# A decay-attention and mixture-of-experts kernel: the state sum as a product with the identity, the router's constants and choices at another place, another first load, and the last group in two pieces

## Chip, cores and metric

The kernel runs on one core of one Trainium2 chip. The metric is the device time of one execution in microseconds (us), as the median of several executions.

## The reference

Two parts follow one another. The first is a linear attention with a complex decay (4 batches, 8 heads, 768 tokens, 48 features a head). The second is a mixture of 8 experts in which each of the 3072 tokens goes to one expert, in the order of the logits, and each expert takes at most 384 tokens.

```python
mag = np.sqrt(a_re * a_re + a_im * a_im)
scale = np.minimum(mag, 0.999) / (mag + 1e-06)
a_re_n, a_im_n = (a_re * scale, a_im * scale)
for t in range(S):
    new_re = ar * S_re - ai * S_im
    new_im = ar * S_im + ai * S_re
    S_re, S_im = (new_re + kv, new_im)
    y[:, :, t] = np.einsum('bhd,bhde->bhe', q[:, :, t], S_re)
...
logits = x @ w_gate
order = np.argsort(-logits.flatten())
for idx in order:
    tok, e = (int(idx) // E, int(idx) % E)
    if assigned[tok] >= 0 or counts[e] >= cap:
        continue
    assigned[tok] = e
    counts[e] += 1
for e in range(E):
    h = np.maximum(x[assigned == e] @ w1[e], 0.0)
    out[assigned == e] = h @ w2[e]
```

## The kernel before

**Attention in chunks.** The tokens of a batch are cut into six chunks of 128. A *unit* is one chunk with all 8 heads, so there are 24 units, 0 to 23; batch 3 is units 18 to 23. In the code `i` is the unit and `cc` its place in the batch (0 to 5). Three units are a *group* (8 groups, 0 to 7; groups 6 and 7 are batch 3). For a whole group `elementwise` works the decays out: squares, logarithms, exponentials and sines on ScalarE (ACT), products, prefix sums (the scans `zi` and `neg`) on VectorE (DVE), with tiles `ar`, `ai`, `s`, `p`, `neg`, `zi`, `CS`, `kq`. `CUTS` lets a group be done in pieces; before, group 0 alone is (one chunk, then two). `PLAN` says, for each piece, in which of the alternating loads of ACT's function tables its four stages lie.

**Rotation and restacking.** `turns` multiplies keys and then queries of a unit by cosine and sine: two DVE instructions `f<-kq,CS` of 768 elements, the second of which makes the unit ready. `stack` then issues eight transfers `KQ<-f` on the queue of SyncE (SP), which take the parts of `f` to the layout that TensorE (PE) needs.

**A unit on PE.** `unit` makes the scores `sc`, which DVE masks (`am`, two instructions a unit); for `cc` below 5 it transposes the keys (`kp`, copied by ACT to `kt`) and multiplies them with the values into `U`, the chunk's own contribution to the state. Before, each head's product is 96 columns wide, of which 48 are its own. For `cc` of 1 to 4, DVE adds the state of the chunks ahead (`tmp<-U,W`) and multiplies the sum with the chunk's decay (`W<-tmp,KQ`); for `cc` of 0 one instruction `W<-U,KQ` does it. Two tiles `W` take turns. `mix` makes `y` from `am` and the values and from the queries and the state; ACT copies it to `xT`, PE turns it and multiplies it with the gate's weights in the same step (`xp<-pick,xT`), ACT copies `x` out to memory `xd`, and DVE reduces the logits (`lg<-xp`).

**Router.** After a batch, `best` chooses the best expert for the batch's six tiles of tokens (five DVE instructions over 48 elements, the first `top<-lg`, the last `oh<-q,qm`). The last batch's lot is done in `Router.scale`, behind attention. `Router.constants` is a list of small pieces (`masks`, `levels`, and five `level`s of four tiny DVE instructions on two partitions, `sa`, `sb`, `sb`, `steps`), handed to `attention` as `later`. With the last logits the search for each expert's threshold starts (`find`, tiles `ind`, `cnt`, `thr`), and then the experts' products (`acc`).

**What sets the order.** In attention every piece of work is an `Op` with an engine, a cost and a priority: `at` (the unit's number, or near it) plus an offset for its kind from the table `OFF`. `in_order` plays these Ops through a list scheduler, which on each engine takes the ready Op of the lowest priority, and emits them in that order; an idle engine takes whatever is ready. All engines then work strictly in this order, the SP queue too. The functions `dve`, `dve2`, `sca` and the numbers in `op(...)` are the costs by which it plans. The experts' part has a planner of its own, which the change doesn't touch. The instructions carry line 131, that of a helper, so they are told apart by their tiles.

Of the kernel before, what the change touches and what calls it, by code (L numbers as in the profile page):

```python
# [24 lines left out]
GC = 3  # L25
# [24 lines left out]
def constants(nc, con, z, w_gate):  # L50
    v, g = nc.vector, nc.gpsimd

    def t(n, shape, dt=F32):
        x = con.tile(shape, dt, name=n)
        setattr(z, n, x)
        return x

    jp = t("jp", [128, 128], I32)
    g.iota(jp, pattern=[[1, 128]], base=0, channel_multiplier=-1)
    v.tensor_scalar(t("ident", [128, 128]), jp, 0.0, None, op0=OP.is_equal)  # L60
    v.tensor_scalar(t("mask", [128, 128]), jp, 0.0, None, op0=OP.is_ge)
# [12 lines left out]
    t("cidx", [128, NT])  # L74
    t("pid", [128, 1])
    pick = t("pick", [128, 4, 104])
    v.memset(pick, 0.0)
    for s in range(2):
        r = slice(64 * s, 64 * s + 48)
        v.tensor_copy(pick[r, :, 48 * s:48 * s + 48], z.ident[r, None, r].to_broadcast([48, 4, 48]))  # L80
        nc.sync.dma_start(pick[r, :, 96:104], w_gate[:, s].rearrange("p d e -> d p e"))
    t("lg", [128, NT, E])
    t("top", [128, NT])
    t("qm", [128, NT])
    t("oh", [128, NT, E], BF)
    t("ext", [128, 2, B])
# [149 lines left out]
def attention(nc, real, tc, z, q, k, a_re, a_im, v_tok, xd, later):  # L236
# [35 lines left out]
        return o  # L272

    def dve(n):
        return n / 960 + 0.069

    def scan_(n):
        return n * 2.15 / 960 + 0.06

    def dve2(n):  # L280
        return n / 1920 + 0.069

    def sca(n, bias=False):
        return n / 1200 + (0.187 if bias else 0.093)

    def pool(n):
        return n / 460 + 0.08
# [53 lines left out]
    def elementwise(gi, j, at):  # L341
# [114 lines left out]
    def unit(i):  # L456
# [11 lines left out]
        for hh in range(2):  # L468
            def scores(hh=hh):
                sc = ps.tile([128, 4, 128], F32, name="sc", bufs=2)  # L470
                mine["sc", hh] = sc
                for h in range(4):
                    nc.tensor.matmul(sc[:, h], KQ()[:, hh * 4 + h, :128], KQ()[:, hh * 4 + h, 128:256], start=True, stop=True)

            def mask(hh=hh):
                a = wk.tile([128, 4, 128], F32, name="am", bufs=4)
                v.tensor_tensor(a, mine["sc", hh], z.mask[:, None].to_broadcast([128, 4, 128]), op=OP.mult)
                mine["am", hh] = a
            op(("SC", i, hh), "pe", 0.875, at - 0.5, scores, KD + [("MK", i - 1, hh)])
            op(("MK", i, hh), "dve", 0.602, at, mask, [("SC", i, hh), ("MX", i - 2)])  # L480
        if cc < 5:
            for hh in range(2):
                def flip(hh=hh):
                    kp = ps.tile([128, 4, 96], F32, name="kp", bufs=2)
                    mine["kp", hh] = kp
                    for h in range(4):
                        nc.tensor.transpose(kp[:, h], KQ()[:, hh * 4 + h, :128], z.ident[:96, :96])

                def copy(hh=hh):
                    if "kt" not in mine:  # L490
                        mine["kt"] = wk.tile([128, 8, 96], F32, name="kt")
                    nc.scalar.activation(mine["kt"][:, hh * 4:hh * 4 + 4], mine["kp", hh], AF.Copy)
                op(("FL", i, hh), "pe", 0.36, at - 0.45, flip, KD + [("KC", i - 1, hh), ("KC", i - 2, hh)])
                op(("KC", i, hh), "act", 0.38, at, copy, [("FL", i, hh), ("ST", i - 2), ("ST", i - 3)])
# [12 lines left out]

            def nxt():
                return W[(cc + 1) % 2][:, :384].rearrange("p (a b) -> p a b", a=8)
            if cc:  # L510
                def add_():
                    tmp = wk.tile([96, 8, 48], F32, name="tmp", bufs=1)
                    mine["tmp"] = tmp
                    v.tensor_tensor(tmp.rearrange("p a b -> p (a b)"), mine["U"][:, :384], W[cc % 2][:, :384], op=OP.add)
                op(("UA", i), "dve", 0.469, at - 0.1, add_, [("ST", i), ("WM", i - 1), ("WM", i - 2)])
                op(("WM", i), "dve", 0.47, at, lambda: v.tensor_tensor(nxt(), mine["tmp"], gate(), op=OP.mult),
                   [("UA", i), ("MX", i - 1)])
            else:
                op(("UA", i), "dve", 0.469, at - 0.1,
                   lambda: v.tensor_tensor(nxt(), mine["U"][:, :384].rearrange("p (a b) -> p a b", a=8), gate(), op=OP.mult),  # L520
                   [("ST", i), ("MX", i - 1), ("WM", i - 2), ("UA", i - 2), ("MX", i - 2)])
                made["WM", i] = made["UA", i]

        def mix():
            Wc = W[cc % 2]
# [40 lines left out]
        op(("MX", i), "pe", 2.2 if cc else 1.18, at, mix,  # L566
           [("MK", i, 0), ("MK", i, 1), ("lv", gi), ("XC", i - 1)] + ([("WM", i - 1)] if cc else []))
        op(("XC", i), "act", 0.478, at - 0.1, evac, [("MX", i), ("FN", i - 2)])
        op(("FN", i), "pe", 0.70, at + 0.6, turn, [("XC", i), ("XE", i - 2), ("LR", i - 2)])
        op(("XE", i), "act", 0.41, at, out, [("FN", i), ("XS", i - 2)])  # L570
        op(("XS", i), "dma", 0.546, at, store, [("XE", i)])
        op(("LR", i), "dve", 0.13 if i % 6 < 5 else 0.98, at, logits, [("FN", i)])

    def load(key, cost, at, fn, deps=()):
        op(key, "dma", cost, at, fn, deps)
# [803 lines left out]
```

## Time and profile before

Three executions took 545.6, 545.8 and 547.11 us, median 545.8. The profile is of a further execution.

| | us |
|---|---|
| the profiled execution's own time | 550.18 |
| its span, first to last instruction | 548.4 |
| busy PE / DVE / ACT / GpSimd (POOL) | 445.6 / 437.1 / 276.5 / 72.9 |
| mean granted TensorE clock | 0.923 |

The page's rows of tenths cut the span into 40 slices of 13.7 us. Row "PE" is the share in which a product was under way, "PEclk" the TensorE clock granted (9 and above is full, 5 is half). A timeline row is: start, duration, engine, line, instruction, tiles written and read, shape, count, and in brackets the idle time ahead of it with what ended it. A windows row is: the stretch, its length, and for each engine its busy time and its instructions, then the granted clock, the share of the DMA engines and the GB/s. A row of the groups ends in the busy time of all and the mean ns of one. SPq and ACTq rows are the issue of transfers. On PE most single-precision products stand as two records, so x16 are eight products.

### The profile page before, as it was taken

The numbers are of one execution on the slowest core, as the hardware profiler recorded it, in microseconds if no ns is written. First come the engines' busy times: TensorE is split into PE (matmuls) and PEld (weight loads), VectorE is DVE, ScalarE is ACT, GpSimd is POOL, SyncE is SP. The second block draws the span as 40 slices with busy tenths as digits, with TensorE's granted clock in tenths as the row PEclk, the third lists the DMA queues.
The fourth block names the chain that finished last, engine by engine and source line by source line (L and its number), as shares of the span: only waits on it lengthen the run. The fifth ranks groups of instructions, "written<-read, shape, count | busy, mean of one in ns | idle before, by whom it ended". The sixth has DMA issues, their size and how long they took to land. (4 is left out here: it accounts for less than half of the span.)

```text
span 548.4 us, 9215 instructions
## 1 busy us (share of the span) xinstructions
PE 445.6 (81%) x3383; PEld 392.6 (72%) x3383; DVE 437.1 (80%) x1267; ACT 276.5 (50%) x422; POOL 72.9 (13%) x87
## 2 busy tenths in 40 slices
PE   0005997699679967995489899999999999999994
PEld 0005996599678856994375458887889888999993
DVE  7999999979899989944667768889899898965240
ACT  5997579828887688322012513244172432834231
POOL 1000000000000000000121311332132223460102
PEclk9999999579859995998569999999999999999999
DMA  8625867578756885541071513245062431950001
GB/s 240 234 76 140 240 200 240 140 193 215 247 155 178 242 276 154 136 120 45 0 274 48 208 47 131 78 177 221 30 244 73 159 130 39 393 189 16 30 14 43
DMA packets 47596, 82.47 MB, mean 150 GB/s; under 512 B 5568, under 2 KB 43200, under 8 KB 45504
## 3 DMA queue, kind: packets, MB, share of 16 engines
q1 hardware_dynamic: 38720, 42.57, 27.2%
q0 software_dynamic: 5376, 34.61, 16.9%
q10 hardware_dynamic: 3456, 4.72, 2.5%
q8 instruction: 26, 0.43, 0.3%
q14 instruction: 18, 0.15, 0.1%
HBM read 53.49 MB, written 9.44 MB: 115 GB/s over the span
## 5 line engine op out<-in xcount | busy, mean ns | idle before, releaser
L131 PE MATMUL sc<-KQ 96*128 96x128 f32 x384 | 60.3, 317 | 41.6 <-DMA KQ<-f 40.7
L131 PEld LDWEIGHTS sc<-KQ 96*128 96x128 f32 x384 | 55.2, 226 | 44.0 <-DMA KQ<-f 41.6
L131 ACT ACTIVATE hh<-acc 128x384 fp32r<-128x384 f32 (+1 forms) x64 | 30.6, 490 | 75.2 <-PE acc L131 75.0
L131 PE MATMUL acc<-w2h,hl 128*128 128x384 f32 x168 | 55.1, 346 | 0.0
L131 PE MATMUL acc<-w2l,hh 128*128 128x384 f32 x168 | 54.9, 345 | 0.0
L131 PE MATMUL acc<-w2h,hh 128*128 128x384 f32 x168 | 54.4, 343 | 0.0
L131 PE MATMUL acc<-xh,w1h 128*128 128x384 f32 x168 | 53.6, 347 | 0.3 <-DVE idx L131 0.2
L131 PE MATMUL acc<-xl,w1h 128*128 128x384 f32 x168 | 53.1, 345 | 0.0
L131 PE MATMUL acc<-xh,w1l 128*128 128x384 f32 x168 | 52.6, 343 | 0.0
L131 POOL DMA_INDIRECT w1t<-in_w,eidx x8 | 8.8, 1099 | 312.4 <-DVE of L131 269.3
L131 ACT ACTIVATE ot<-acc 128x384 f32<-128x384 f32 x24 | 11.8, 492 | 70.7 <-PE acc L131 55.8
L131 DVE TENSOR_TENSOR f<-kq,CS 128x768 f32<-128x768 f32 x48 | 43.7, 949 | 0.9 <-ACT CS L131 0.9
L131 DVE SCALAR_TENSOR_TENSOR hl<-acc,hh 128x384 fp32r<-128x384 f32 x56 | 30.4, 551 | 15.9 <-ACT hh L131 15.3
L131 PE MATMUL y<-am,V 128*64 128x128 f32 x384 | 38.0, 288 | 3.0 <-DVE am L131 2.0
L131 DVE TENSOR_TENSOR ind<-m,thr 128x768 bf16<-128x768 f32 (+1 forms) x40 | 33.7, 849 | 6.9 <-PE thr L131 6.6
L131 PE MATMUL kp<-ident,KQ 96*128 96x96 f32 x160 | 25.0, 301 | 15.7 <-DMA KQ<-f 9.5
L131 POOL DMA_INDIRECT out<-ot,idx x24 | 25.3, 1053 | 93.2 <-ACT ot L131 82.9
L131 DVE TENSOR_TENSOR am<-sc,mask 128x512 f32<-128x512 f32 x48 | 31.5, 680 | 6.2 <-PE sc L131 6.1
L131 PE MATMUL U<-V,kt 128*96 128x96 f32 x320 | 35.2, 270 | 0.9 <-DVE tmp L131 0.9
L131 POOL DMA_INDIRECT xg<-xd,idx x24 | 28.1, 1172 | 57.1 <-DVE idx L131 29.4
L131 PEld LDWEIGHTS U<-V,kt 128*96 128x96 f32 x320 | 33.1, 184 | 2.7 <-issue 1.2
L131 PE MATMUL xp<-pick,xT 112*128 112x104 f32 x192 | 25.9, 285 | 10.7 <-ACT xT L131 8.5
(195 smaller groups left out, 1082.7 us busy)
## 6 DMA issues: line engine op xcount, KB each, us to landing
KQ<-f SPq DMA_DIRECT2D x192, 96.4 KB, 2.2
V<-in_v SPq DMA_DIRECT2D x8, 576.0 KB, 4.8
kq<-in_k SPq DMA_DIRECT2D x8, 576.0 KB, 6.6
kq<-in_q SPq DMA_DIRECT2D x8, 576.0 KB, 7.8
xd<-x ACTq DMA_DIRECT2D x24, 192.0 KB, 3.0
ai<-in_a_im SPq DMA_DIRECT2D x7, 576.0 KB, 4.4
ar<-in_a_re SPq DMA_DIRECT2D x7, 576.0 KB, 5.1
ai<-in_a_im SPq DMA_DIRECT2D x1, 384.0 KB, 3.6
```

Of the source, the lines that this page charges most:

```text
L131: r = f(*a, **k)
```

## The change

Five things in the code, and the table of offsets.

- **State sum on PE.** `state` multiplies each head with its own 48 columns, into a `U` of 384 columns, and leaves the sum open; for `cc` of 1 to 4 a new Op `CA` multiplies the old state `W` (96 x 384) with the identity into the same `U`. DVE's `tmp<-U,W` is gone, and `W<-U,KQ` reads `U` for every unit. `U` is then free only when `W<-U,KQ` is done.
- **Router.** The priority of `later` goes from 3.0 to 23.0, and `best` for the first three batches becomes one Op over 18 tiles (144 elements), `BE`, with priority 25.
- **Loads.** A group's `ar` no longer waits for its `ai` in the plan, and the two small transfers of `w_gate` go from SP's queue to GpSimd's.
- **Last group.** `CUTS` cuts group 7 into its first two chunks and its last one, and `PLAN` has ten entries with 20 table loads instead of nine with 22.
- **Planning costs** are somewhat higher for DVE and ACT, and every offset in `OFF` has another value.

```diff
-        nc.sync.dma_start(pick[r, :, 96:104], w_gate[:, s].rearrange("p d e -> d p e"))
+        g.dma_start(pick[r, :, 96:104], w_gate[:, s].rearrange("p d e -> d p e"))
...
-CUTS = {0: [(0, 1), (1, GC)]}
+CUTS = {0: [(0, 1), (1, GC)], 7: [(0, 2), (2, GC)]}
...
     def dve(n):
-        return n / 960 + 0.069
+        return n / 960 + 0.1
...
-        add("la", "dma", dma(128 * N3 * 4), load_a(gi, j, "ar", a_re), free("ar", ["F1", "F3", "F4"], gi) + k_("li"))
+        add("la", "dma", dma(128 * N3 * 4), load_a(gi, j, "ar", a_re), free("ar", ["F1", "F3", "F4"], gi))
...
             def state():
-                Wc = W[cc % 2]
-                U = ps.tile([96, 432], F32, name="U")
+                U = ps.tile([96, 384], F32, name="U")
                 mine["U"] = U
                 for h in range(8):
-                    nc.tensor.matmul(U[:, h * 48:h * 48 + 96], mine["kt"][:, h], v_[:, c, h * 48:h * 48 + 96],
-                                     start=True, stop=True)
-            op(("ST", i), "pe", 1.33, at - 0.2, state, [("KC", i, 0), ("KC", i, 1), ("lv", gi), ("UA", i - 1), ("UA", i - 2)])
+                    nc.tensor.matmul(U[:, h * 48:h * 48 + 48], mine["kt"][:, h], v_[:, c, h * 48:h * 48 + 48],
+                                     start=(h == 0), stop=(h == 7 and not cc), skip_group_check=True)
+
+            def carry():
+                nc.tensor.matmul(mine["U"], z.ident[:96, :96], W[cc % 2][:, :384], start=False, stop=True,
+                                 skip_group_check=True)
+            op(("ST", i), "pe", 1.33, at - 0.2, state, [("KC", i, 0), ("KC", i, 1), ("lv", gi), ("WM", i - 1), ("WM", i - 2)])
+            if cc:
+                op(("CA", i), "pe", 0.65, at - 0.1, carry, [("ST", i), ("WM", i - 1), ("WM", i - 2)])
+            else:
+                made["CA", i] = made["ST", i]
...
-            if cc:
-                def add_():
-                    tmp = wk.tile([96, 8, 48], F32, name="tmp", bufs=1)
-                    mine["tmp"] = tmp
-                    v.tensor_tensor(tmp.rearrange("p a b -> p (a b)"), mine["U"][:, :384], W[cc % 2][:, :384], op=OP.add)
-                op(("UA", i), "dve", 0.469, at - 0.1, add_, [("ST", i), ("WM", i - 1), ("WM", i - 2)])
-                op(("WM", i), "dve", 0.47, at, lambda: v.tensor_tensor(nxt(), mine["tmp"], gate(), op=OP.mult),
-                   [("UA", i), ("MX", i - 1)])
...
+            op(("WM", i), "dve", 0.52, at,
+               lambda: v.tensor_tensor(nxt(), mine["U"].rearrange("p (a b) -> p a b", a=8), gate(), op=OP.mult),
+               [("CA", i), ("MX", i - 1), ("CA", i - 1)])
...
-                if i + 1 < NT:
-                    best(nc, z, wk, z.lg[:, r], z.top[:, r], z.qm[:, r], z.oh[:, r])
...
-        op(("later", n), "dve", 0.6, 3.0, lambda fn=fn: fn(nc), [("later", n - 1)])
-    made["LR", 5].deps.append(made["later", len(later) - 1])
+        op(("later", n), "dve", 1.0, NT - 1.0, lambda fn=fn: fn(nc), [("later", n - 1)])
+
+    def choices():
+        r = slice(0, NT - 6)
+        best(nc, z, wk, z.lg[:, r], z.top[:, r], z.qm[:, r], z.oh[:, r])
+    op(("BE", 0), "dve", 1.5, NT + 1.0, choices, [("LR", i) for i in range(NT - 6)] + [("later", len(later) - 1)])
...
-PLAN = [(0, 0, 1, 3), (0, 2, 1, 3), (2, 4, 3, 5), (4, 6, 5, 7), (6, 8, 7, 9), (8, 10, 9, 11), (10, 12, 11, 13), (14, 16, 15, 17), (18, 20, 19, 21)]
+PLAN = [(0, 0, 1, 3), (0, 2, 1, 3), (2, 4, 3, 5), (4, 6, 5, 7), (6, 8, 7, 9), (8, 10, 9, 11), (10, 12, 11, 13), (12, 14, 13, 15), (14, 16, 15, 17), (16, 18, 17, 19)]
```

Where rows stand now is shown at three places. In these rows a shape like 128x3x128 is partitions by elements, and x2 is a run of two alike.

The start of SP's queue (`V` are the values, `kq` keys and queries), before:

```order
L131 DMA ai<-in_a_im 128x3x128
L131 DMA ai<-in_a_im 128x3x256
L81 DMA pick<-in_w_gate 48x4x8 x2
L131 DMA V_114<-in_v 128x3x384
L131 DMA ar<-in_a_re 128x3x128
L131 DMA ar<-in_a_re 128x3x256
```

and in the changed kernel:

```order
L131 DMA ar<-in_a_re 128x3x128
L131 DMA ar<-in_a_re 128x3x256
L131 DMA ai<-in_a_im 128x3x128
L131 DMA ai<-in_a_im 128x3x256
L131 DMA V_114<-in_v 128x3x384
```

`ar` now goes first, and the gate's weights have left the queue.

The start of DVE's real work in the changed kernel. Before, all five `level`s stand ahead of the first row that needs a load, `p<-ar,ai`:

```order
L131 TENSOR_SCALAR start<-jf 1x32
L131 TENSOR_SCALAR pidm<-pid 32x1
L131 TENSOR_SCALAR neg<-ar 128x3x128
L131 TENSOR_SCALAR sa<-jf 2x32
L131 TENSOR_SCALAR sb<-jf 2x32
L131 TENSOR_TENSOR sb<-sb,sa 2x32
L131 SCALAR_TENSOR_TENSOR steps<-sb,row,sa 2x32
L131 TENSOR_SCALAR neg<-ar 128x3x256
```

The `level`s now stand singly among the first groups' work, all of them within the first two groups, though their priority says the end of attention.

DVE around the rotations of units 18 to 20, before (the first row of three holds both of unit 18 and one of unit 19; `zi`, `p`, `neg` and the second `kq` are group 7's):

```order
L131 TENSOR_TENSOR f<-kq,CS 128x6x128 x3
L131 TENSOR_SCALAR zi<-s_1755 128x1152
L131 TENSOR_TENSOR f<-kq,CS 128x6x128
L131 TENSOR_TENSOR p<-p,s_1806 128x1152
L131 SCALAR_TENSOR_TENSOR zi<-zi,s_1755 128x128 x9
L131 SCALAR_TENSOR_TENSOR neg<-p,tl,neg 128x384 x3
L131 TENSOR_TENSOR f<-kq,CS 128x6x128
L131 TENSOR_TENSOR kq<-kq,zi 128x1152
L131 TENSOR_SCALAR neg<-neg 128x1152
L131 TENSOR_TENSOR f<-kq,CS 128x6x128
```

and in the changed kernel (the rows of `p` are group 7's first piece; `W` and `am` belong to units 16 and 17):

```order
L131 TENSOR_TENSOR f<-kq,CS 128x6x128 x3
L131 TENSOR_TENSOR W_112<-U,KQ 96x384
L131 TENSOR_TENSOR am<-sc,mask 128x512 x2
L131 TENSOR_TENSOR f<-kq,CS 128x6x128
L131 TENSOR_TENSOR p<-p,s_1666 128x3x256
L131 TENSOR_TENSOR f<-kq,CS 128x6x128 x2
```

The prefix sums and most of group 7's other work now stand behind unit 20's second rotation.

DVE ahead of the last two rotations (unit 23's) in the changed kernel; the `W` is unit 20's:

```order
L131 TENSOR_SCALAR neg<-neg 128x3x128
L131 TENSOR_TENSOR W_112<-U,KQ 96x384
L131 TENSOR_TENSOR kq<-kq,s_1706 128x3x128
L131 TENSOR_REDUCE top<-lg 128x18
L131 TENSOR_TENSOR q_2204<-lg,top 128x144
L131 TENSOR_TENSOR q_2204<-q_2204,wd 128x144
L131 TENSOR_REDUCE qm<-q_2204 128x18
L131 TENSOR_TENSOR oh<-q_2204,qm 128x144
L131 TENSOR_TENSOR f<-kq,CS 128x6x128 x2
```

Unit 23's rotations now wait, in DVE's order, for a `W` that waits for PE, and for the choices of the first 18 tiles.

More of the change, by code (lines that the diff above doesn't have):

```diff
@@ L280, in dve2 @@
     def dve2(n):
-        return n / 1920 + 0.069
+        return n / 1920 + 0.11
     def sca(n, bias=False):
-        return n / 1200 + (0.187 if bias else 0.093)
+        return n / 1200 + (0.23 if bias else 0.14)
     def pool(n):
@@ L478, in mask @@
                 mine["am", hh] = a
-            op(("SC", i, hh), "pe", 0.875, at - 0.5, scores, KD + [("MK", i - 1, hh)])
-            op(("MK", i, hh), "dve", 0.602, at, mask, [("SC", i, hh), ("MX", i - 2)])
+            op(("SC", i, hh), "pe", 0.9, at - 0.5, scores, KD + [("MK", i - 1, hh)])
+            op(("MK", i, hh), "dve", 0.64, at, mask, [("SC", i, hh), ("MX", i - 2)])
         if cc < 5:
@@ L492, in copy @@
                     nc.scalar.activation(mine["kt"][:, hh * 4:hh * 4 + 4], mine["kp", hh], AF.Copy)
-                op(("FL", i, hh), "pe", 0.36, at - 0.45, flip, KD + [("KC", i - 1, hh), ("KC", i - 2, hh)])
-                op(("KC", i, hh), "act", 0.38, at, copy, [("FL", i, hh), ("ST", i - 2), ("ST", i - 3)])
+                op(("FL", i, hh), "pe", 0.34, at - 0.45, flip, KD + [("KC", i - 1, hh), ("KC", i - 2, hh)])
+                op(("KC", i, hh), "act", 0.44, at, copy, [("FL", i, hh), ("ST", i - 2), ("ST", i - 3)])
             def state():
-                Wc = W[cc % 2]
-                U = ps.tile([96, 432], F32, name="U")
+                U = ps.tile([96, 384], F32, name="U")
                 mine["U"] = U
                 for h in range(8):
-                    nc.tensor.matmul(U[:, h * 48:h * 48 + 96], mine["kt"][:, h], v_[:, c, h * 48:h * 48 + 96],
-                                     start=True, stop=True)
-            op(("ST", i), "pe", 1.33, at - 0.2, state, [("KC", i, 0), ("KC", i, 1), ("lv", gi), ("UA", i - 1), ("UA", i - 2)])
+                    nc.tensor.matmul(U[:, h * 48:h * 48 + 48], mine["kt"][:, h], v_[:, c, h * 48:h * 48 + 48],
[8 more added lines that the diff above has]
+                made["CA", i] = made["ST", i]
             def gate():
@@ L509, in nxt @@
                 return W[(cc + 1) % 2][:, :384].rearrange("p (a b) -> p a b", a=8)
-            if cc:
-                def add_():
-                    tmp = wk.tile([96, 8, 48], F32, name="tmp", bufs=1)
-                    mine["tmp"] = tmp
-                    v.tensor_tensor(tmp.rearrange("p a b -> p (a b)"), mine["U"][:, :384], W[cc % 2][:, :384], op=OP.add)
-                op(("UA", i), "dve", 0.469, at - 0.1, add_, [("ST", i), ("WM", i - 1), ("WM", i - 2)])
-                op(("WM", i), "dve", 0.47, at, lambda: v.tensor_tensor(nxt(), mine["tmp"], gate(), op=OP.mult),
-                   [("UA", i), ("MX", i - 1)])
[L518 to L522, printed above, removed]
+            op(("WM", i), "dve", 0.52, at,
+               lambda: v.tensor_tensor(nxt(), mine["U"].rearrange("p (a b) -> p a b", a=8), gate(), op=OP.mult),
+               [("CA", i), ("MX", i - 1), ("CA", i - 1)])
         def mix():
@@ L563, in logits @@
                 v.tensor_reduce(z.ext[:, 1, b:b + 1], lg, op=OP.min, axis=AX.X)
-                if i + 1 < NT:
-                    best(nc, z, wk, z.lg[:, r], z.top[:, r], z.qm[:, r], z.oh[:, r])
-        op(("MX", i), "pe", 2.2 if cc else 1.18, at, mix,
+        op(("MX", i), "pe", 1.9 if cc else 1.0, at, mix,
            [("MK", i, 0), ("MK", i, 1), ("lv", gi), ("XC", i - 1)] + ([("WM", i - 1)] if cc else []))
-        op(("XC", i), "act", 0.478, at - 0.1, evac, [("MX", i), ("FN", i - 2)])
-        op(("FN", i), "pe", 0.70, at + 0.6, turn, [("XC", i), ("XE", i - 2), ("LR", i - 2)])
-        op(("XE", i), "act", 0.41, at, out, [("FN", i), ("XS", i - 2)])
+        op(("XC", i), "act", 0.54, at - 0.1, evac, [("MX", i), ("FN", i - 2)])
+        op(("FN", i), "pe", 0.9, at + 0.6, turn, [("XC", i), ("XE", i - 2), ("LR", i - 2)])
+        op(("XE", i), "act", 0.46, at, out, [("FN", i), ("XS", i - 2)])
         op(("XS", i), "dma", 0.546, at, store, [("XE", i)])
-        op(("LR", i), "dve", 0.13 if i % 6 < 5 else 0.98, at, logits, [("FN", i)])
+        op(("LR", i), "dve", 0.15 if i % 6 < 5 else 0.45, at, logits, [("FN", i)])
     def load(key, cost, at, fn, deps=()):
@@ L626 @@
 START = dict(pe=0.0, act=0.6, dve=1.5, pool=3.4, dma=0.0)
-OFF = {"A1": 5.6974, "F1": -7.9403, "F10": -7.0891, "F11": -2.5142, "F2": 4.603, "F3": 2.2139, "F4": 2.5395, "F5": -0.7373, "F6": -7.499, "F7": -8.0, "F8": 8.0, "F9": -4.5957, "FL": -8.0, "FL<": -0.67, "FN": 7.9979, "G1": -0.9278, "G2": -0.7621, "G3": 0.005, "G4": 2.5464, "G5": -8.0, "K": 0.9248, "KC": 8.0, "LR": 8.0, "MK": 3.115, "MX": 3.0055, "N0": -8.0, "N1": -6.1077, "N2": -1.1451, "P0": -1.533, "R0": -1.808, "R1": -6.8663, "R2": -0.3699, "R3": 5.5431, "R4": -2.409, "R5": -7.3329, "S": -8.0, "SC": -7.6492, "SC<": -8.0, "ST": 4.3481, "ST<": -5.7794, "T1": 1.9301, "T2": -8.0, "T3": 2.462, "TL": 3.4506, "UA": -5.175, "UA<": -8.0, "WM": 8.0, "XC": -2.3796, "XC<": 3.7972, "XE": -0.9541, "XS": 8.0, "la": -5.2264, "later": -1.1817, "li": -4.9185, "lk": 6.1616, "lv": 4.0153, "RK": -0.8502, "RQ": -0.8125, "table": -3.9707}
+OFF = {"A1": 6.5218, "F1": -3.963, "F10": -8.0, "F11": -3.7643, "F2": 8.0, "F3": 3.4146, "F4": 6.2286, "F5": -2.6336, "F6": -7.5201, "F7": 2.1619, "F8": -1.0245, "F9": -8.0, "FL": -8.0, "FL<": -7.3946, "FN": 8.0, "G1": 8.0, "G2": -1.285, "G3": 6.3021, "G4": -5.8232, "G5": -3.7953, "K": 0.0172, "KC": -8.0, "LR": 4.482, "MK": -0.7872, "MX": 7.0247, "N0": 0.2966, "N1": -8.0, "N2": -0.2657, "P0": -5.8009, "R0": 6.9605, "R1": 1.4172, "R2": -2.4071, "R3": -0.3573, "R4": 4.9463, "R5": -1.815, "S": -8.0, "SC": 1.5433, "SC<": 3.9494, "ST": -0.4983, "ST<": 8.0, "T1": 0.0502, "T2": -6.6124, "T3": -0.6944, "TL": -2.0259, "UA": -4.4369, "UA<": 5.2541, "WM": -6.1886, "XC": -0.2695, "XC<": 5.8251, "XE": 1.7266, "XS": 4.1758, "la": -8.0, "later": 0.9443, "li": -6.5411, "lk": 8.0, "lv": 7.3515, "RK": -2.6027, "RQ": -2.5432, "table": 7.641, "CA": -5.0223, "BE": 6.7757}
 CHAIN = ("scalar", "vector", "tensor", "gpsimd", "sync")
```

## The prediction

> **What bounds the kernel now.** I read the rows of tenths on the page first, to cut the span into stages.
>
> ```profile
> span 548.4 us, 9215 instructions
> PE   0005997699679967995489899999999999999994
> DVE  7999999979899989944667768889899898965240
> PEclk9999999579859995998569999999999999999999
> ```
>
> DVE is full up to slice 16 (219 us), PE only afterwards. The windows of attention show the change of hands.
>
> ```profile
> 172.00:201.40 29.40, 26.19 (x312) 24.22 (x312) 27.33 (x51) 21.85 (x27) 0.00 (x0) 1.00 0.75 234
> 201.40:227.00 25.60, 19.58 (x149) 17.57 (x150) 24.72 (x42) 18.82 (x23) 0.00 (x0) 0.73 0.61 167
> 227.00:253.40 26.40, 25.48 (x312) 24.11 (x308) 11.57 (x30) 6.96 (x14) 0.00 (x0) 1.00 0.38 102
> ```
>
> Behind the length stand the busy times of PE, its weight loads, DVE, ACT and GpSimd. Up to 227 DVE has work nearly all the time; then PE has 26 us left to do, alone. So attention is a DVE stage with a PE tail, and the tail is as long as batch 3 comes late to PE. The third view is the timeline there.
>
> ```profile
> 200.49 2.69 DVE L131 TENSOR_TENSOR f<-kq,CS 128x768 f32<-128x768 f32 x3
> 215.25 0.95 DVE L131 TENSOR_TENSOR f<-kq,CS 128x768 f32<-128x768 f32 x1
> 220.69 3.55 DVE L131 TENSOR_TENSOR f<-kq,CS 128x768 f32<-128x768 f32 x4
> 253.18 0.19 DVE L131 TENSOR_REDUCE lg<-xp 128x8 f32<-128x32 f32 x1 [0.85 <-ACT x L131]
> 36.96 16.58 SPq L131 DMA_DIRECT2D KQ<-f  x24
> 202.34 36.26 SPq L131 DMA_DIRECT2D KQ<-f  x48
> KQ<-f SPq DMA_DIRECT2D x192, 96.4 KB, 2.2
> ```
>
> Unit 18's second rotation ends at 202.3 (200.49 and two of the three in 2.69), unit 20's at 216.2, unit 21's at 222.4. SP issues the transfers of the six units in one run, from 202.34 to 238.6. One unit's eight take 5.5 us in an earlier run (16.58/3) and land 2.2 later. Attention ends with the last logits at 253.4. The 295.0 us of router and experts behind that are the same rows in the same order in both programs and read nothing that the change makes later, so I leave them as they are.
>
> **The change, term by term**, against the profiled execution.
>
> *The start.* DVE's first row that needs a load waits for `ar`.
>
> ```profile
> 0.75 0.97 SPq L131 DMA_DIRECT2D ai<-in_a_im  x2
> 3.27 1.02 SPq L131 DMA_DIRECT2D ar<-in_a_re  x2
> 3.43 0.52 ACT L131 ACTIVATE s<-ai 128x384 f32<-128x384 f32 x1 [1.40 <-DMA ai<-in_a_im]
> 8.66 0.56 DVE L131 SCALAR_TENSOR_TENSOR p<-ar,ai 128x384 f32<-128x384 f32 x1 [1.48 <-DMA ar<-in_a_re]
> 2.10 0.60 DVE L80 COPY pick<-ident 48x192 f32<-48x192 f32 x2
> 1.03 0.79 POOL L131 MEMSET W<- 96x400 f32 x2
> 2.78 0.23 POOL L131 IOTA jf<- 2x32 f32 x1
> L131 POOL DMA_INDIRECT xg<-xd,idx x24 | 28.1, 1172 | 57.1 <-DVE idx L131 29.4
> ```
>
> What is issued first is there at 3.43, so DVE could begin at 3.4 instead of 8.66. But GpSimd now issues the two transfers of `w_gate`, which wait for `pick`, ahead of its constants, and DVE's `start<-jf` stands ahead of its first `neg<-ar`. This trace has no such issue on GpSimd. The nearest row is the indirect transfer, 1.17 us. Two of them behind `pick` at 2.7 end at 5.0, and the 2.0 us of constants (1.03 to 3.01) bring DVE to 7.0; with nothing for them it is 3.4. I take 6.0, near the row: **-2.7** (-5.3 to -1.7).
>
> *DVE's work ahead of unit 18.*
>
> ```profile
> 189.02 0.55 DVE L131 TENSOR_TENSOR tmp<-U,W 96x384 f32<-96x384 f32 x1
> 189.49 0.75 DVE L131 TENSOR_SCALAR neg<-neg 128x1152 int32<-128x1152 int32 x1
> 228.59 0.19 DVE L131 TENSOR_REDUCE top<-lg 128x6 f32<-128x48 f32 x1
> 229.54 0.21 DVE L131 TENSOR_TENSOR oh<-q,qm 128x48 bf16<-128x48 f32 x1
> 3.26 0.16 DVE L131 TENSOR_SCALAR sa<-jf 2x32 f32<-2x32 f32 x1
> 6.94 0.24 DVE L131 SCALAR_TENSOR_TENSOR steps<-sb,row,sa 2x32 bf16<-2x32 f32 x1
> ```
>
> A sum `tmp` holds DVE for 0.47 us (to the next start); batches 0 to 2 have 12: **-5.6**. A lot of choices takes 1.15 (228.59 to 229.75), and two lots stood ahead: **-2.3**. The five levels took 3.9 us (3.26 to 7.18) in the wait for the first load; in the new order they stand behind it: **+3.9**. Adding start-to-start times row by row through both orders leaves +0.5 for other pieces of group 7 now ahead. Together -6.2: unit 18's second rotation ends near **196.1**.
>
> ACT has two table loads fewer; it was not the last to be waited for at these rows, and I count nothing for them.
>
> *Units 18 to 20.* From there to unit 20's second rotation the new order has four rotations (0.87 each), one `W` (0.47), two masks (0.60 each) and a `p` (0.87): 6.0 us, so **202.1** instead of 216.2. The three sets of transfers go out in one run: unit 18 lands at 203.8 (5.5 and 2.2), unit 20 at 214.3 instead of 223.8.
>
> *Unit 21 on.* Splitting group 7 adds instructions, and the 18 tiles' choices move ahead of unit 23's rotations; unit 21's second rotation has 1.3 us less of work ahead than before, so with the start 218.4 instead of 222.4. SP then issues 24 transfers in 16.6 us, to 235.0, landed at 237.2.
>
> *PE's tail.*
>
> ```profile
> sum 43.50, PE 41.89 PEld 39.56 DVE 29.38 ACT 18.55 POOL 0.00; mean PE 6.98 PEld 6.59 DVE 4.90 ACT 3.09 POOL 0.00
> 209.00:216.00 7.00, 5.63 (x28) 5.26 (x29) 7.00 (x10) 6.11 (x7) 0.00 (x0) 0.50 0.62 173
> 221.80 1.60 PE L131 MATMUL U<-V,kt 128*96 128x96 f32 x16
> 223.23 1.06 PE L131 MATMUL xp<-pick,xT 112*128 112x104 f32 x8
> 224.13 0.82 PE L131 MATMUL kp<-ident,KQ 96*128 96x96 f32 x8
> 224.79 1.98 PE L131 MATMUL sc<-KQ 96*128 96x128 f32 x16
> 248.54 0.44 PE L131 MATMUL y<-am,V 128*64 128x128 f32 x4
> 287.99 1.46 PE L131 MATMUL acc<-xh,w1t 128*128 128x384 f32 x4
> 250.45 2.03 PE L131 MATMUL xp<-pick,xT 112*128 112x104 f32 x16
> 356.91 0.25 PE cnt L131 x6
> ```
>
> From 209 to 252.5, six units took 41.9 us of PE, the first at half clock. `U` takes 1.43 (221.80 to 223.23, where the next product starts). With 48 columns the trace has none: half is 0.72, nothing saved is 1.43. Six `cnt` products of 32 columns, each with its own 128 weights, take 0.25, or 0.04 a load; with two loads a product that gives 0.67. I take 0.75, so -0.7 in five units. The identity product is four times `U`'s width; the same width in single precision takes 0.73 (four records, 1.46), in four units +2.9. Net -0.6 (-0.8 to +2.9). PE can begin at 203.2, as unit 18's first heads land, and is done 41.3 later: **244.5**. By SP's run it is 237.2 and the last unit's mask, `y`, copy, turn and logits: 1.2 and the 4.8 from 248.54 to 253.37, **243.2**. The later of the two, about 244.4, sets the end: **-9.0**. In batches 0 to 2 PE's net change (12 x 0.73 more, 15 x 0.7 less) lies beside DVE's work. `U` has one buffer, now free only after `W`; between one unit's sum and the next unit's `U` stand a `y` (1.9, 248.54 to 250.45) and mostly `sc` on PE, which cover the 0.5 us of `W`; without that cover PE would lose these 0.5 us in each of four units.
>
> The Trainium skill, page "TensorE: Matmul & The Clock Gate", section "LDWEIGHTS (loading the stationary operand)", has a load last its columns divided by 1.2, in ns. For 96 columns, loaded twice, that is an estimated 1.28 us for eight products, so `U` would save only 0.15 and the tail would end 2.7 later, -6.3 in all. The trace speaks against it: the four `kp` products load 128 columns twice each and take 0.66 (224.13 to 224.79), where the rule gives 0.85.
>
> *Sum.* 550.18 - 9.0 = 541.2 for a profiled execution. It stood 4.4 above the median of 545.8, so the median becomes **536.8**.
>
> **Rivals.**
>
> *The `W` rows wait for PE in the tail.* Unit 20's `W` stands ahead of unit 23's rotations. After unit 20 lands at 214.3, PE owes `sc`, `y`, `U`, a turn and the sum, 6.5 us at full clock, so 220.8, and DVE comes there at 221.5. At half clock it is 227.3, and the last rotations come 5.8 later: 232 instead of 226, landed at 240, end 246. With 1 us in each earlier batch the end is near 249, the time **541.5**. For it: the clock of 0.73 from 201 to 227. Against it: PE has two units waiting by then, and from 227 the clock is 1.00.
>
> *GpSimd holds up the start.* If each transfer takes twice the 1.17, `start<-jf` comes at 9.4, 0.7 after today's start instead of 2.7 ahead: **540.2**. The trace shows no such issue beside DVE's copies. The Trainium skill, page "SBUF — State Buffer", section "SBUF: two separate sides", warns of just this: transfers issued from GpSimd starve while DVE copies single-precision tiles, 3.1 us instead of 0.62; by an estimate of 5 us more than nothing for the two it would give about the same time, and no run here shows it so far.
>
> *Slower: every `W` waits for the product, from batch 0.* The state's sum leaves DVE but DVE must now wait, in its order, until PE has done `U` and the sum.
>
> ```profile
> DVE W L131 <- PE U L131: 4.0, 2, 3.1
> sum 165.40, PE 135.65; mean PE 33.91
> ```
>
> Before 227, the `W` that read `U` directly, one a batch, waited 4.0 us in all, 3.1 the longest; averaged over four, 1.0 each. If the 12 new ones wait 1.3 each (4.0 over the three of batches 0 to 2), DVE loses 15.6 us and the time is 536.8 + 15.6 = **552.4**. It is slower than before from 0.75 us each on (9.0/12). For it: at half clock `U` and the sum take 3 us. Against it: in the new order 5 to 9 us of other DVE rows lie between one `W` and the next, and from 36 to 201.4 PE has 29.8 us free.
>
> *It doesn't do what it says.* SP's queue has loads of `V` and `kq` ahead of unit 18's transfers; if one waits for unit 14, those go out no earlier, and the time is **545.8**.
>
> **How the numbers follow.** Forecast 0.50 (its own terms span 532 to 540), tail wait 0.20, GpSimd 0.12, slower 0.13, nothing 0.05. The range takes in the first three, from 531 to 543.5. Faster by over 0.3% (about what a measurement here can tell from no change) are the first three, less a little for their near ends: 0.81; same 0.06; slower 0.13.
>
> **What would show it.** Right: DVE's first row with a load at about 6; unit 18's second rotation near 196 and unit 20's near 202; SP's last run ended by 235; `U` near 0.75 us for eight at full clock; PE without long waits from 204; last logits near 244; router and experts 295 us. Wrong: DVE rows `W` with idle from PE above 0.75 us on average; a wait for `w_gate`; `U` still at 1.4; or PE at half clock beyond 212.

## The result: 1% slower, and where the time went

The changed kernel takes **552.74 us** (552.49 to 554.86, four runs), the kernel before 546.45 on the same chip (545.6 to 548.11): a ratio of **1.0102**, 95% interval 1.0076 to 1.0129. 536.8 was forecast, with a range up to 543.5. The profiled execution took 552.71 and is thus a typical one.

The rows of tenths on the page of the changed kernel come first.

```profile
span 550.9 us, 9282 instructions
PE   0019995899879899998369999999999999999994
DVE  8998889968997967964576888889899898965240
PEclk9999997559956958999559999999999999999998
```

PE mostly has 8s and 9s from the fourth slice on, while DVE, which was full up to the sixteenth, has gaps. In slices 8, 9 and 15 PE has 8 or 9 and its clock row has 5: PE is busy because it is slow. Two windows give the size, one from the middle of attention and one that the prediction used; the columns are as there, and the last three are the granted clock, the DMA share and GB/s.

```profile
100.00:200.00 100.00, 92.06 (x738) 84.49 (x738) 87.33 (x153) 72.62 (x89) 0.00 (x0) 0.74 0.69 192
201.40:227.00 25.60, 25.36 (x232) 22.79 (x232) 19.31 (x40) 12.63 (x22) 0.00 (x0) 0.83 0.60 168
```

The same first window in the kernel before:

```profile
100.00:200.00 100.00, 87.01 (x854) 81.19 (x856) 91.52 (x172) 71.92 (x87) 0.00 (x0) 0.84 0.73 209
```

In these 100 us PE is busy for 5 us more and shows 116 product records fewer, and DVE's busy time falls from 91.5 to 87.3. From 201 to 227 PE is busy nearly throughout (25.36 of 25.60; before 19.58) and DVE for 19.3 us (before 24.7). What DVE waits for stands in the waits of the changed kernel from 3 to 227 us (who waited for whom; us in all, times, longest).

```profile
DVE am L131 <- PE sc L131: 13.5, 9, 4.0
DVE W L131 <- PE U L131: 5.1, 4, 3.6
DVE W L131 <- PE y L131: 2.0, 1, 2.0
```

That is 20.6 us. Before, it was the 4.0 us of `W` and 0.9 us of `tmp`. (The waits of the logits' rows, 1.7 us here and 1.3 before, are left out.) Most of it isn't the wait for the state (`W`) but for the scores (`sc`), ahead of a mask `am` that stands in DVE's row. The timeline shows such places, at 56.81, 116.15 and 204.15, and what came of them.

```profile
1.78 1.41 POOL L81 DMA_DIRECT2D pick<-in_w_gate  x2 [0.69 <-DVE ident L60]
5.10 0.40 DVE L131 TENSOR_SCALAR neg<-ar 128x384 f32<-128x384 f32 x1
49.84 2.79 PE L131 MATMUL U<-V,kt 128*96 128x48 f32 x16
52.44 1.51 PE L131 MATMUL kp<-ident,KQ 96*128 96x96 f32 x8
56.81 0.69 DVE L131 TENSOR_TENSOR am<-sc,mask 128x512 f32<-128x512 f32 x1 [3.04 <-PE sc L131]
101.72 2.85 PE L131 MATMUL U<-V,kt 128*96 128x48 f32 x16
104.36 1.51 PE L131 MATMUL kp<-ident,KQ 96*128 96x96 f32 x8
112.92 1.49 PE L131 MATMUL U<-W,ident 96*96 96x384 f32 x2
116.15 0.69 DVE L131 TENSOR_TENSOR am<-sc,mask 128x512 f32<-128x512 f32 x1 [3.14 <-PE sc L131]
204.15 0.69 DVE L131 TENSOR_TENSOR am<-sc,mask 128x512 f32<-128x512 f32 x1 [3.96 <-PE sc L131]
204.76 2.69 DVE L131 TENSOR_TENSOR f<-kq,CS 128x768 f32<-128x768 f32 x3
206.60 17.28 SPq L131 DMA_DIRECT2D KQ<-f  x24
220.38 1.47 PEld L131 LDWEIGHTS U<-V,kt 128*96 128x96 f32 x16
220.49 1.48 PE L131 MATMUL U<-V,kt 128*96 128x48 f32 x16
221.81 0.84 PE L131 MATMUL kp<-ident,KQ 96*128 96x96 f32 x8
222.49 1.08 PE L131 MATMUL sc<-KQ 96*128 96x128 f32 x8
223.54 1.56 PE L131 MATMUL U<-V,kt 128*96 128x48 f32 x16
225.06 1.16 PE L131 MATMUL sc<-KQ 96*128 96x128 f32 x8
231.79 16.23 SPq L131 DMA_DIRECT2D KQ<-f  x24
259.02 0.19 DVE L131 TENSOR_REDUCE lg<-xp 128x8 f32<-128x32 f32 x1 [0.18 <-PE xp L131]
```

Eight heads of `U` (16 records, two a product) take 2.64 us at half clock (101.72 to 104.36) and 1.32 at full clock (220.49 to 221.81); the prediction had 0.75. The mask at 204.15 waits 3.96 us for scores, and unit 18's second rotation stands right behind it: it ends at 206.6 instead of the forecast 196.1, SP's last run begins at 231.79 and ends at 248.0 instead of 235, and the last logits come at 259.2 instead of 244.4. Against before (253.4) attention is 5.8 us longer, which accounts for nearly all of the 6.3 us between the medians. Router and experts took 291.7 us in this execution (550.9 - 259.2); the 295.0 of before came from an execution 3.7 us above its median. In ten of the eleven other kernels below it took 290.0 to 292.6, so that execution's excess lies mostly there and not in attention.

The clock by windows of 3.41 us, in the first long stretch at half clock of the changed kernel, from where PE is busy throughout:

```profile
101.79:105.20 3.41, 3.41 (x23) 3.33 (x22) 3.41 (x4) 3.40 (x4) 0.00 (x0) 0.50 0.51 127
105.20:108.61 3.41, 3.41 (x19) 3.41 (x18) 3.09 (x7) 3.25 (x4) 0.00 (x0) 0.50 0.60 154
108.61:112.02 3.41, 3.41 (x23) 3.41 (x23) 3.41 (x10) 2.47 (x3) 0.00 (x0) 0.50 0.87 235
112.02:115.43 3.41, 3.41 (x15) 2.75 (x15) 0.99 (x2) 0.98 (x2) 0.00 (x0) 0.50 1.04 376
115.43:118.84 3.41, 3.41 (x22) 3.19 (x22) 2.69 (x4) 0.00 (x0) 0.00 (x0) 0.50 0.25 93
```

PE has work in every moment of five windows and still gets half the clock. So being busy in the records is not what brings the clock back. That gave the **theory** (A in the expectations): a product of 48 columns takes as long as one of 96, because the load of its 128x96 weights sets the time (the row `LDWEIGHTS` at 220.38 lasts 1.47 us). In that time the array streams only half as many columns, and the clock stays at half for longer. PE falls behind, and DVE, which works strictly in order, stands at the masks. **Rivals**: the price by columns, as predicted; the added identity product itself; the other order that the new offsets give.

### The profile page after: what moved, and what is told of

Its sections match the earlier page's. It is cut to its first block, busy times and chain, and to the rows that moved or that the text cites. A ratio compares the mean times of both kernels' runs of the same rounds, so it can differ in the third digit from the quotient of the medians.

```text
span 550.9 us, 9282 instructions
## 1 busy us (share of the span) xinstructions
PE 465.3 (84%) x3415; PEld 408.1 (74%) x3415; DVE 431.6 (78%) x1255; ACT 277.2 (50%) x432; POOL 74.5 (14%) x89
## 5 line engine op out<-in xcount | busy, mean ns | idle before, releaser
L131 PEld LDWEIGHTS sc<-KQ 96*128 96x128 f32 x384 | 60.9, 243 | 5.4 <-issue 3.9
L131 PE MATMUL sc<-KQ 96*128 96x128 f32 x384 | 63.3, 330 | 0.0
L131 PEld LDWEIGHTS kp<-ident,KQ 96*128 96x128 f32 x160 | 20.5, 180 | 53.2 <-DVE f L131 37.4
L131 PEld LDWEIGHTS U<-V,kt 128*96 128x96 f32 x320 | 38.0, 205 | 1.9 <-ACT kt L131 1.3
L131 PE MATMUL U<-V,kt 128*96 128x48 f32 x320 | 38.7, 286 | 0.7 <-ACT kt L131 0.7
L131 PE MATMUL y<-am,V 128*64 128x128 f32 x384 | 39.3, 297 | 0.0
L131 ACT ACTIVATE xT<-y 128x512 f32<-128x512 f32 x24 | 14.2, 594 | 42.7 <-PE y L131 42.7
```

Source lines behind the costliest of these rows:

```text
L131: r = f(*a, **k)
```

## Experiments

### The width of U, and nothing else

First the kernel before with `U` cut to 48 columns; its order of instructions is that of before.

```diff
-                U = ps.tile([96, 432], F32, name="U")
+                U = ps.tile([96, 384], F32, name="U")
...
-                    nc.tensor.matmul(U[:, h * 48:h * 48 + 96], mine["kt"][:, h], v_[:, c, h * 48:h * 48 + 96],
+                    nc.tensor.matmul(U[:, h * 48:h * 48 + 48], mine["kt"][:, h], v_[:, c, h * 48:h * 48 + 48],
```

> The kernel before with each head's U product 48 columns wide instead of 96, in the same order of instructions, nothing else changed. By the price by columns (as predicted): U falls from about 1.35 to 0.75 us, 4 to 6 of them on the path at the end, 542.5-544.5 against 546.5. Theory A (no time saved, array left idle, clock lower for longer): U's rows stay at 1.3 to 1.5 us at full clock, half-clock stretches get longer by one to three windows of 3.41 us, 547-552. Theory C (width does nothing): 546-547 with the same half-clock stretches.

Measured: 558.07 us, ratio **1.0177** (1.0125 to 1.0228). Half the columns make the kernel before 9 us slower, more than theory A expected (547 to 552). Its window from 100 to 200, and then the same work in both, from 3 us to unit 18's first rotation, before and with 48 columns:

```profile
100.00:200.00 100.00, 86.67 (x771) 81.23 (x771) 90.23 (x168) 69.61 (x83) 0.00 (x0) 0.74 0.66 186
```

```profile
3.00:200.49 197.49, 135.09 (x1304) 125.16 (x1304) 184.08 (x351) 150.67 (x179) 0.18 (x7) 0.90 0.69 202
3.00:209.37 206.37, 145.94 (x1304) 136.12 (x1304) 184.91 (x351) 151.30 (x178) 0.18 (x7) 0.88 0.66 194
```

From 100 to 200 the clock falls from 0.84 to 0.74, the value of the changed kernel, though the identity product, the new offsets and everything else are missing. The same 1304 product records keep PE busy for 10.9 us more, and the same 351 rows of DVE, which take no longer, need 8.9 us more, 6.2 of them as longer waits for PE. The price by columns has the wrong sign.

The same in the other direction, the changed kernel with 96 columns again:

```diff
-                U = ps.tile([96, 384], F32, name="U")
+                U = ps.tile([96, 432], F32, name="U")
...
-                    nc.tensor.matmul(U[:, h * 48:h * 48 + 48], mine["kt"][:, h], v_[:, c, h * 48:h * 48 + 48],
-                                     start=(h == 0), stop=(h == 7 and not cc), skip_group_check=True)
+                    nc.tensor.matmul(U[:, h * 48:h * 48 + 96], mine["kt"][:, h], v_[:, c, h * 48:h * 48 + 96],
+                                     start=True, stop=(not cc), skip_group_check=True)
...
```

> The changed kernel with each head's U product 96 columns wide again, in the same order of instructions (the identity product then adds onto the first 384 columns). Theory A (the narrow products save no time, since a weight load stands ahead of each, and they leave the array idle for half of that time, so that the granted clock stays at half for longer): U's rows at full clock stay at 1.3 to 1.5 us, the half-clock stretches (98 to 121, 153 to 176, 194 to 208 in the changed kernel) get shorter, and the time falls from 552.7 to 546-551. Theory B (the price by columns, as predicted): 8 products go from 0.75 to 1.4 us, four to six of them on TensorE's path at the end, 555-557. Theory C (it is the order of the work, width does nothing): 552-553.5, with the half-clock stretches as they were.

Measured: 539.99 us, **0.9844** (0.9801 to 0.9888). This is below theory A's own 546 to 551: the width alone turns a loss of 1.0% into a gain of 1.6%. Here overlapping heads each start their columns anew and the identity product follows; the state so formed is not the reference's sum, so the time alone is read from it. Its window from 100 to 200:

```profile
100.00:200.00 100.00, 87.17 (x857) 78.19 (x856) 92.57 (x160) 73.31 (x91) 0.00 (x0) 0.91 0.74 212
```

Two runs at 64 columns, one in the order of before, where only the widths of the product and of `U` change, and one in that of the changed kernel, whose new lines are:

```diff
+                U = ps.tile([96, 8, 64], F32, name="U")
...
+                    nc.tensor.matmul(U[:, h], mine["kt"][:, h], v_[:, c, h * 48:h * 48 + 64],
...
+                nc.tensor.matmul(mine["U"][:, :, :48], z.ident[:96, :96], W[cc % 2][:, :384].rearrange("p (a b) -> p a b", a=8), start=False, stop=True,
...
```

> The kernel before with each head's U product 64 columns wide instead of 96, in the same order. 48 wide stood at 1.0177, 96 at 1. If the clock follows the streaming share, 1.007 to 1.014; if 64 columns fill the time of a weight load and that is enough, 0.998 to 1.003; if all under 96 is alike, 1.015 to 1.020.

> The changed kernel with U laid out as 8 heads of 64 columns (one PSUM bank), each head's product 64 columns wide, the identity product and W's row on the first 48 of each; the same order of instructions. Measured so far, against the kernel before on the same chip: 48 wide 1.0102 and 96 wide 0.9844. If the granted clock follows how long the array streams for each weight load, 64 lies between, 0.993 to 1.004, with a clock from 100 to 200 us of 0.77 to 0.87 (0.74 at 48, 0.91 at 96). If only streaming that covers the whole load counts, near 0.985. If anything under 96 is as bad as 48, 1.008 to 1.012.

Measured: before with 64 columns **1.0056** (1.0041 to 1.0071), the changed kernel with 64 **1.0000** (0.9966 to 1.0035), with clocks of 0.82 and 0.78 in the window from 100 to 200. In both orders the time falls step by step from 48 to 64 to 96 columns: 1.0177, 1.0056, 1 in that of before, and 1.0102, 1.0000, 0.9844 in that of the change. The clock rises with it, 0.74, 0.82, 0.84 and 0.74, 0.78, 0.91. The 64 in the order of the change lies in the range expected for a clock that follows the streaming share; that in the order of before lies between two of the ranges (up to 1.003, from 1.007).

### A wide U that forms the right state

The `U` of before has 432 columns, in which heads 96 wide overlap by 48. `V` has 48 columns of zeros behind its 384. So each head can stream its own 48 columns and these zeros, which add nothing to the next head's columns. The new lines:

```diff
+                    vz = v_[:, c, h * 48:432].rearrange("p (a b) -> p a b", b=48)[:, 0:9 - h:8 - h]
+                    nc.tensor.matmul(U[:, h * 48:h * 48 + 96].rearrange("p (a b) -> p a b", b=48), mine["kt"][:, h], vz,
+                                     start=(h == 0), stop=(h == 7 and not cc), skip_group_check=True)
...
```

> The changed kernel with each head's U product 96 columns wide, its second 48 read from V's zeroed padding, so that they add zero to the next head's columns and the state is formed as in the changed kernel; the same order. If the array's streaming time sets the granted clock, whatever the values: 0.982 to 0.988, like the wide kernel (0.9844), with a clock of 0.88 to 0.93 from 100 to 200 us. If zeros do not count as work, or the wide kernel gained by its other values: 1.005 to 1.012, with 0.72 to 0.77.

> The kernel with the zero-padded U again (0.9856 before), for a profile of an undisturbed execution. If streaming sets the clock, whatever the values: a granted clock of 0.88 to 0.93 from 100 to 200 us, DVE's waits for `sc` and `U` in that stretch under 6 us in all (20 in the changed kernel), the last `lg` at 243 to 247, and 0.982 to 0.988.

Measured: 540.48 us, **0.9856** (0.9825 to 0.9887), and the second time 539.36, **0.9822** (0.9751 to 0.9894). This is the version that forms the right state and beats both kernels: its arithmetic, order and instruction count are those of the changed kernel, plus 48 columns of zeros a head. Windows and waits (3 to 227) of the second run:

```profile
100.00:200.00 100.00, 86.31 (x816) 77.52 (x814) 89.47 (x155) 70.72 (x87) 0.00 (x0) 0.88 0.73 208
```

```profile
DVE am L131 <- PE sc L131: 6.9, 8, 2.1
DVE W L131 <- PE U L131: 0.9, 2, 0.5
```

With a clock of 0.88 instead of 0.74 DVE's waits for PE up to 227 fall from 20.6 to 7.8 us, by 12.8, and the last logits come 12.0 us earlier, at 247.2. So zeros keep the clock up too, nearly as well as the wide kernel's values (0.91). The time lies in the expected range and the clock at its lower edge, but the last logits come 0.2 us behind theirs. And the expectation laid the 20 us between 100 and 200, which was wrong: in that stretch it is 10.7 in the changed kernel and 7.0 here (under 6 was expected), and the rest goes at single places before and behind it. The timeline of this kernel:

```profile
49.66 1.60 PE L131 MATMUL U<-V,kt 128*96 128x96 f32 x16 [0.35 <-ACT kt L131]
53.97 0.69 DVE L131 TENSOR_TENSOR am<-sc,mask 128x512 f32<-128x512 f32 x1 [0.20 <-PE sc L131]
195.05 2.69 DVE L131 TENSOR_TENSOR f<-kq,CS 128x768 f32<-128x768 f32 x3
196.90 15.85 SPq L131 DMA_DIRECT2D KQ<-f  x24
201.05 1.82 DVE L131 TENSOR_TENSOR f<-kq,CS 128x768 f32<-128x768 f32 x2
207.84 1.47 PEld L131 LDWEIGHTS U<-V,kt 128*96 128x96 f32 x16
207.95 1.52 PE L131 MATMUL U<-V,kt 128*96 128x96 f32 x16
209.31 0.83 PE L131 MATMUL kp<-ident,KQ 96*128 96x96 f32 x8
217.41 1.81 DVE L131 TENSOR_TENSOR f<-kq,CS 128x768 f32<-128x768 f32 x2
219.25 15.81 SPq L131 DMA_DIRECT2D KQ<-f  x24
247.00 0.19 DVE L131 TENSOR_REDUCE lg<-xp 128x8 f32<-128x32 f32 x1 [0.18 <-PE xp L131]
```

The first two rows of it show one such place. Up to 48 us both kernels' rows stand within 0.2 us of each other. Then the changed kernel's `U` at 49.84 takes 2.79 us, at half speed, and DVE's mask waits 3.04 for the scores; here the `U` at 49.66 takes 1.60, at full speed, and the mask waits 0.20 and comes 2.8 us earlier. At full clock `U` takes 1.36 us here with 96 columns (207.95 to 209.31), against 1.32 with 48: the width is nearly free. The weight loads say why: their row lasts 1.47 us at 96 columns (207.84) as at 48 (220.38 in the changed kernel), about as long as the products.

### The identity product

```diff
             def carry():
-                nc.tensor.matmul(mine["U"], z.ident[:96, :96], W[cc % 2][:, :384], start=False, stop=True,
-                                 skip_group_check=True)
+                pass
...
```

> The changed kernel with the 20 identity products left out (so the carried state is left out of the output), everything else in the same order. The products take 0.65 to 0.74 us each at full clock and 1.3 to 1.5 at half. Theory A (clock and weight loads of U): the products fill the array well, so without them only their own time goes: 0.7 x 4 to 6 at the end, 548-551. Theory B (the product ahead of each W is what DVE waits for, DVE's waits for `sc`, `U` and `y` of about 20 us in all come from it): 541-546. Theory C (the order): 551-553.

> The changed kernel with U 96 columns wide and no identity product (the carried state is left out), otherwise the same order. The products' price where the clock is good. If only those on TensorE's path at the end count, as predicted (0.73 each, four to six): 0.7 to 0.8% under the wide kernel with products (0.9844), so 0.976 to 0.979. If they are hidden beside DVE: 0.983 to 0.986. If they cost what they cost at 48 columns (1.0102 against 0.9918): 0.965 to 0.968.

Measured: at 48 columns without the product 544.83 us, **0.9918** (0.9887 to 0.9948), 1.8% under the changed kernel, whose ratio is from another chip; at 96 columns without it 535.59, **0.9748** (0.9719 to 0.9776), 1.0% under the wide kernel. (The products are 16, four a batch, and not the 20 of the expectation.) The first lies in theory B's range (541 to 546), and 3 us under theory A's. Its windows and waits say how much of B holds:

```profile
100.00:200.00 100.00, 92.59 (x754) 88.39 (x755) 89.60 (x155) 72.44 (x88) 0.00 (x0) 0.72 0.72 208
```

```profile
DVE am L131 <- PE sc L131: 11.6, 9, 2.0
DVE W L131 <- PE y L131: 1.2, 1, 1.2
```

Without the product the clock is no better (0.72), and 12.8 of DVE's 20.6 us of waits stay, so it is neither what holds the clock down nor the source of most waits, as B had it. But where PE is behind, the product's 1.49 us at half clock (112.92 in the changed kernel) is on the path: 7.8 us of waits go with it, and with the forecast's 2.9 for the four products in the tail that makes about the 10 us measured (1.8%). With the wide `U` the product costs 1.0%, some 5 us, give or take 0.5%; the prediction's 2.9 lies within that. In the traces, one execution each, the last logits come 8.8 us earlier without the product at 48 columns (250.4 for 259.2) and 1.9 earlier at 96 (242.5 for 244.4). This suggests that its price depends on the clock; the ratios alone, with their intervals, hardly tell 1.8% from 1.0%.

### Single parts undone or made alone

In four more kernels a part is undone or made alone. Here the planner places the work anew, with offsets that belong to another set of work. The kernel before with the early start alone:

```diff
-        nc.sync.dma_start(pick[r, :, 96:104], w_gate[:, s].rearrange("p d e -> d p e"))
+        g.dma_start(pick[r, :, 96:104], w_gate[:, s].rearrange("p d e -> d p e"))
...
-        add("la", "dma", dma(128 * N3 * 4), load_a(gi, j, "ar", a_re), free("ar", ["F1", "F3", "F4"], gi) + k_("li"))
+        add("la", "dma", dma(128 * N3 * 4), load_a(gi, j, "ar", a_re), free("ar", ["F1", "F3", "F4"], gi))
```

The zero-padded kernel with the late start has the same two lines the other way round. The kernel before with the identity product alone, `U` zero-padded, has the change's `carry` and `WM`, the zero-padded `state`, and in `OFF` one more entry, `"CA": -5.175`:

```diff
+                op(("CA", i), "pe", 0.65, at - 0.1, carry, [("ST", i), ("WM", i - 1), ("WM", i - 2)])
...
```

The changed kernel with the sum on DVE has before's `state`, sum and `WM`; of these the sum's lines:

```diff
+                    v.tensor_tensor(tmp.rearrange("p a b -> p (a b)"), mine["U"][:, :384], W[cc % 2][:, :384], op=OP.add)
+                op(("UA", i), "dve", 0.469, at - 0.1, add_, [("ST", i), ("WM", i - 1), ("WM", i - 2)])
...
```

> The kernel before with the change's start alone: the gate's weights loaded by GpSimd's queue and the real parts not held behind the imaginary ones (the planner then places some transfers and rows otherwise). The first real row of DVE comes 3.6 us earlier in the changed kernel than before. If DVE bounds the stretch up to unit 23 and nothing else moves, the end comes 2.7 to 3.6 us earlier: 0.993 to 0.995. If the gain is taken up by later waits for TensorE at half clock, 0.998 to 1.002.

> The zero-padded kernel with the start of before: the gate's weights on SP's queue and the real parts behind the imaginary ones (the planner then places some rows otherwise). If the early start is worth what it measured at DVE's first rows, 2.7 to 3.6 us of the gain: 0.991 to 0.994. If it is worth nothing at the end, as in the kernel before alone (1.0067): 0.984 to 0.987.

> The kernel before with the state sum alone made by the identity product, U 96 wide with the zero padding; start, router constants, choices, group 7, costs and offsets as before (the product's own offset is that which the sum had). If the sum saves its 12 DVE rows on the bounding engine (5.6 us) less four products at the end (2.9): 0.994 to 0.996. If the order that goes with it decides, as in the changed kernel with the sum on DVE (1.0124): 1.003 to 1.015.

> The changed kernel with the state sum of before put back (U 96 wide, the sum with W by a `tmp` row on DVE), the other parts of the change as they are: the early loads, the router constants and choices at the end, group 7 in two pieces, and the changed costs and offsets, which set another order than before's. As predicted (the sum by product saves 5.6 us of DVE): 557-559. Theory A or B (the state sum by product is what costs): 541-548. Theory C (the order that the new costs and offsets give is what costs, whoever makes the sum): 550-556.

Measured, in this order: **1.0067** (1.0034 to 1.01), **1.0201** (1.0154 to 1.0248), **1.0296** (1.0251 to 1.0341), **1.0124** (1.0091 to 1.0157). Only the last lies in an expected range, that of the order. The clock isn't to blame: it is 0.85, 0.86, 0.85 and 0.89 from 100 to 200, as high as before (0.84). The timeline of the late start says what is.

```profile
212.98 0.29 DVE L131 TENSOR_REDUCE top<-lg 128x18 f32<-128x144 f32 x1
214.55 4.42 DVE L131 TENSOR_TENSOR f<-kq,CS 128x768 f32<-128x768 f32 x5
216.40 36.14 SPq L131 DMA_DIRECT2D KQ<-f  x48
```

The 18 tiles' choices and pieces of group 7 now stand ahead of unit 18's second rotation, which ends at 216.4 instead of 196.9, and SP's last run ends at 252.5 instead of 235.1. In the other three it ends at 239.4, 245.5 and 243.5, against 238.6 before. So these four price orders and not parts, and what the start, the choices, the sum and group 7 each bring at the end stays open. A test would have to hold the order fixed; none here did.

## Why the prediction was wrong, point by point

**The step that failed** is in PE's tail and in the sentence behind it. "I take 0.75" for a `U` of 48 columns: at full clock it is 1.32 (220.49 to 221.81 in the changed kernel) to 1.52 (223.54 to 225.06), so the bound "nothing saved, 1.43" was the truth. And "In batches 0 to 2 PE's net change (...) lies beside DVE's work": PE's clock was taken as it stood before. The narrow product lowered it from 0.84 to 0.74, PE came behind, and DVE waited 20.6 us for it. The second error is the large one, the 12.0 us between the ends of the changed and the zero-padded kernel (259.2 and 247.2). The first should cost 0.6 to 0.7 us in each of the last units. Whether it does at the end stays open: the zero-padded kernel ends 2.8 us behind the forecast of 244.4, but the wide one, whose `U` takes as long (1.36, 204.66 to 206.02), ends at 244.4. Of the signs of being wrong that the prediction names, "`U` still at 1.4" came true.

The rule of the Trainium skill on the page "TensorE: Matmul & The Clock Gate", section "LDWEIGHTS (loading the stationary operand)", was set aside for the sake of one `kp` row. It makes a load last its columns over 1.2, in ns, an estimated 1.28 for the eight products. `U` measured 1.32 at the least: here the trace agrees with it, though `kp` still goes faster than the rule (0.68, from 221.81 to 222.49 in the changed kernel, against an estimated 0.85). Of the clock the rule says nothing.

**The start** was nearly right: 6.0 forecast for DVE's first row with a load, 5.10 measured (`neg<-ar`). The two transfers hold GpSimd 0.7 us each (1.41 for both, at 1.78), not 1.17, and the rival in which GpSimd holds up the start fell.

**DVE's work and the order** were nearly right, as the zero-padded kernel shows, where PE keeps up better. Unit 18's second rotation ends there at 196.9 (forecast 196.1), unit 20's at 202.9 (202.1), unit 21's at 219.2 (218.4), and SP's run at 235.1 (235.0). Its ratios of 0.9856 and 0.9822 lie about the forecast's 536.8/545.8 = 0.9835. In part errors cancel there: DVE's first row came 0.9 us earlier than forecast, while up to 202 us DVE waits 8.9 us for PE, 2.7 more than before, which the forecast didn't count. Its time is that of the change with the width of `U` left alone, though 0.75 for `U` was wrong there too.

**The slower rival** named 552.4 and the time is 552.7, but that is luck, as its mechanism is a small part of it. It let the 12 new `W` wait 1.3 us each, 15.6 in all. `W` waited 7.1 us in all up to 227, 2.2 more than `W` and `tmp` before; the other 13.5 stand at the masks. The tail rival saw the half clock, but only from 201 on, and not that the change itself would lengthen it.

## What to carry to other kernels

Before a product is made narrower, look whether its weight load already sets its time: if its row lasts as long at half the columns, nothing is saved and the array only streams less. Where the trace shows a granted clock of 0.5 in windows in which PE is busy throughout, columns can be part of what keeps the clock up, as they are here, and a term that is "beside other work" has to be priced at the clock that the change leaves behind. An in-order engine passes such a delay on at the first row that waits for PE, whatever that row is; so the waits of all its rows are read, not only those that the change touches.

## What the runs showed of the hardware

The granted clock stayed at 0.50 in five successive windows of 3.41 us with PE busy for all of each, and padding the products with zeros raised it from 0.74 to 0.88 over 100 us. The Trainium skill, page "TensorE: Matmul & The Clock Gate", section "What's actually happening", gives full clock after one busy window of about 3.4 us. By the busy time of the profile's records the trace here disagrees; how much of a window the array must stream to count as busy, no run here shows, only that 48, 64 and 96 columns a load give rising clocks. And the clock column can't be relied on everywhere. The window from 48 to 57 us of the changed kernel:

```profile
48.00:57.00 9.00, 9.00 (x50) 8.11 (x50) 5.96 (x12) 4.32 (x7) 0.00 (x0) 1.00 0.78 227
```

It says 1.00, while `U` and `kp` take 2.79 and 1.51 us, nearly twice their 1.48 and 0.84 at 220. PE's first product had begun only at 37.4 us, and why the column reads 1.00 there isn't shown; durations are the safer sign.
